# Fused attention and feed-forward: the first weight piece is loaded ahead of everything, and weight conversion runs one piece earlier

## The chip, the cores and the metric

The kernel runs on one core of one Trainium2 chip. The metric is the device time of one execution in microseconds (us). The time before is 648.15 us, the median of three runs (646.57 to 648.39).

## The reference

`B, H, S, D = 4, 8, 768, 64`. Attention looks at a window of keys and at one summary of each block of 32 keys; a feed-forward layer with the Mish function follows. All data are float32.

```python
k_sum = k.reshape(B, H, nb, 32, D).max(axis=3)
v_sum = v.reshape(B, H, nb, 32, D).mean(axis=3)
scores_l = scale * q @ k^T          # kept where |i - j| < 16, else -1e9
scores_s = scale * q @ k_sum^T + log(32)
a = softmax(concat([scores_l, scores_s]))
attn = a @ concat([v, v_sum])                 # (4, 8, 768, 64)
x = attn.transpose(0, 2, 1, 3).reshape(3072, 512)
h = x @ w_in                                   # 512 -> 2048
g = h * tanh(log1p(exp(h)))
out = g @ w_out                                # 2048 -> 512
```

## The kernel before

**Work and tiling.** Tokens are cut into 12 chunks of 256; an attention *unit* is one chunk with one of four pairs of heads, so there are 48 units. Two chunks (512 tokens) make one of six groups of the feed-forward. A group has 16 steps; step i does `ff_in` (12 matmuls into `ph`, L386), Mish on ScalarE (L393), a split of the result into a high part `ah` and a rest `al` (L402, L404), and, two steps later, `ff_out` (12 matmuls into `po`, L414). Every product is made of three matmuls on high and low parts.

**Weights.** Both weight matrices arrive as 64-bit floats and are converted on the chip. They are cut into 16 pieces, taken in turn from `w_in` and `w_out`; I call them p0 to p15. An even piece feeds two `ff_in` steps, an odd one two `ff_out` steps. Each piece goes through five calls, each of which takes the oldest piece that has finished the call before:

- `load_weight` (L122): two loads of 512 KB on SyncE's queue into one of two `stage` buffers. The load of the third piece therefore waits until the first has been begun, and so on, and whatever is queued behind it on SyncE waits with it.
- `begin_weight`: a copy `f` on ScalarE (L134) and two shifts on VectorE (L136, L138). This frees the stage buffer.
- `join_weight`: two operations on VectorE (L146, L148).
- `upper_weight`: the high part `w_hi` on ScalarE (L156).
- `lower_weight`: the low part `w_lo` on VectorE (L163).

**Order.** It is written by hand: every engine takes its instructions in the order of the program. First all loads of the first eight units are issued. Then a loop over u = 0 to 10 treats these units as a pipeline: scores of unit u (`sc` on TensorE, `pr` with L327 on VectorE, exponentials on ScalarE, L331), normalisation of unit u-1 (L341, L342 on VectorE, L343 on GpSimd), the value summary `vm` of unit u-1, the product with the values of unit u-3 (`x_ps`, with `xh` L373 on ScalarE and `xl` L374 on VectorE), and the transposes of unit u-2 (`pt`). `first_key_summary(hp)` (`km`, L242 on VectorE) must come before the scores of unit hp. The calls for the weights are put between these at chosen values of u. Then the main loop runs over the 96 steps; in its first steps it opens with

```python
upper_weight(); join_weight(); begin_weight(); load_weight()
if 0 < i <= NFC:
    waiting.pop(0)()      # al of step i-1
```

and `lower_weight()` follows after `ff_in` and the scores of a step. Later attention units are spread over these steps.

**Before.** In the loop over u the pieces go so: p0 is begun at u=1, joined at 2, lowered at 3; p1 begun at 6, joined at 8, lowered at 9; p2 begun at 8, joined at 10; p3 begun at 10. Step 0 of the main loop joins p3, begins p4, and lowers p2.

Of the kernel before, what the change touches and what calls it, by code (L numbers as in the profile page):

```python
# [30 lines left out]
HP = H // 2  # L31
# [26 lines left out]
def fused_kernel(ctx: ExitStack, tc: tile.TileContext, q0, qk, kt, v0, vw, vs, w_in, w_out, out):  # L58
# [45 lines left out]
    def home(j, part, dtype, name):  # L104

        if j == NW:
            t = stage.tile([P, WB, WP], I64, tag="stage", name=name).bitcast(dtype)
            return t.rearrange("p k f -> p (k f)")[:, :WB * WP]
        pool = const if j < EARLY else late[0]
        return pool.tile([P, WB * WP], dtype, tag=f"w{part}_{j}", name=name, bufs=1)  # L110
# [6 lines left out]
    def load_weight():  # L117
        if weights:
            w, fc = weights.pop(0)
            t = stage.tile([P, WB, WP], I64, tag="stage", name=f"w{w}_{fc}")  # L120
            for k in range(WB):
                nc.sync.dma_start(t[:, k, :], (w_in, w_out)[w][fc + k])  # L122
            loaded.append((w, fc, t))

    def begin_weight():
        if loaded:
            w, fc, t = loaded.pop(0)
            j = order[w, fc]
            flat = t.rearrange("p k f -> p (k f)")
            high = flat.bitcast(U32).rearrange("p (f two) -> p f two", two=2)[:, :, 1]  # L130
            quarter = flat.bitcast(U16).rearrange("p (f four) -> p f four", four=4)
            x = home(j, 0, U32, f"x{w}_{fc}")
            f = home(j + 1, 1, F32, f"f{w}_{fc}")
            nc.scalar.activation(f, high.bitcast(F32), AF.Copy, scale=2.0 ** -OFFSET)  # L134
            half = x.bitcast(U16).rearrange("p (f two) -> p f two", two=2)
            nc.vector.tensor_scalar(out=half[:, :, 0], in0=quarter[:, :, 1], scalar1=13, scalar2=None,  # L136
                                    op0=ALU.logical_shift_right)
            nc.vector.tensor_scalar(out=half[:, :, 1], in0=quarter[:, :, 3], scalar1=SIGN, scalar2=None,  # L138
                                    op0=ALU.bitwise_and)
            begun.append((w, fc, f, x))  # L140
# [64 lines left out]
    def first_keys(hp):  # L205

        ks = keys0[hp] = first_att.tile([P, WIN + S], F32, tag="ks", name=f"ks0_{hp}")
        nc.gpsimd.memset(ks[:, 0:WIN], 0.0)
        nc.sync.dma_start(ks[:, WIN:], kt[0, hp])
        t = first_att.tile([P, CH], F32, tag="q0", name=f"q0_{hp}")  # L210
        nc.sync.dma_start(t, q0[hp])
        t = t.rearrange("p (s q) -> p s q", s=NQ)
        units[0, hp] = {"q": [t, t], "k": ks[:, :CH + 2 * WIN]}

    def first_key_summary(hp):
        key_summary(0, hp, keys0[hp][:, WIN:])

    def window_values(c, hp):
        pool = first_att if c == 0 or (c < CG and hp > 1) else att
        u = units.setdefault((c, hp), {})  # L220
        u["v"] = pool.tile([KA, NQ, P], F32, tag="vw", name=f"vw{c}_{hp}", bufs=HP if pool is first_att else 2)
        nc.sync.dma_start(u["v"][0:KW], vw[c, hp].rearrange("p (s k) -> p s k", s=NQ))

    def block_values(c, hp):
        nc.gpsimd.tensor_copy(units[c, hp]["v"][KW:KA],
                              summary[c // CPB, hp][1].unsqueeze(1).broadcast_to([NB, NQ, P]))

    def second_queries(hp):
        t = first_att.tile([P, NQ, P], F32, tag="q1", name=f"q1_{hp}")
        nc.sync.dma_start(t, qk[1, hp].rearrange("p (s k) -> p s k", s=NQ)[:, :, :P])  # L230
        units[1, hp] = {"q": [t[:, :, h * QT:(h + 1) * QT] for h in range(2)], "k": keys0[hp][:, CH:]}

    def first_values(hp):
        window_values(0, hp)
        t = first_att.tile([P, NR, P], F32, tag="v0", name=f"v0_{hp}", bufs=HP)
        nc.sync.dma_start(t, v0[hp].rearrange("p (j d) -> p j d", d=P))
        units[0, hp]["rest"] = t

    def key_summary(b, hp, keys):

        km = att.tile([P, NB], F32, tag="km", name=f"km{b}_{hp}", bufs=HP)
        nc.vector.reduce_max(km, keys.rearrange("p (n j) -> p n j", j=BLK), axis=AX.X)  # L242
        summary[b, hp] = [km]

    def first_value_summary(hp):

        vm = att.tile([KA, P], F32, tag="vm", name=f"vm0_{hp}", bufs=HP)[KW:KA]
        summary[0, hp].append(vm)
        vwt, t = units[0, hp]["v"], units[0, hp]["rest"]
        ps = att_psum(0, f"vm_ps0_{hp}")  # L250
        for j in range(NQ + NR):
            nc.tensor.matmul(ps[KW:KA, 0:P], *((blocks[0:KW, j, :], vwt[0:KW, j, :]) if j < NQ else
                                               (blocks[:, j, :], t[:, j - NQ, :])),
                             start=(j == 0), stop=(j == NQ + NR - 1))
        nc.scalar.copy(vm, ps[KW:KA, 0:P])
        block_values(0, hp)
# [9 lines left out]
    def att_load_keys(c, hp):  # L266
        t = att.tile([P, NQ, P + KA], F32, tag="qk", name=f"qk{c}_{hp}")
        nc.sync.dma_start(t, qk[c, hp].rearrange("p (s k) -> p s k", s=NQ))
        units[c, hp] = {"qk": t}
# [67 lines left out]
    def att_normalize(group):  # L337
        n = len(group) * NQ
        u = units[group[0]]
        rs = small.tile([P, 2 * NQ], F32, tag="rs", name=f"rs{group[0][0]}_{group[0][1]}")[:, :n]  # L340
        nc.vector.tensor_scalar_add(rs, u["sm"][:, :n], 1e-9)  # L341
        nc.vector.reciprocal(rs, rs)  # L342
        nc.gpsimd.tensor_mul(u["pr"], u["pr"], rs.unsqueeze(2).broadcast_to([P, n, KA]))  # L343
# [11 lines left out]
    def att_values(group):  # L355
        c, hp0 = group[0]
        n = len(group)
        g, half = divmod(c, CG)
        if g not in xs:
            xs[g] = (xp.tile([P, HP, TG], F32R, tag="xh", name=f"xh{g}"),  # L360
                     xp.tile([P, HP, TG], F32R, tag="xl", name=f"xl{g}"))
        xh, xl = (x[:, hp0:hp0 + n, half * CH:(half + 1) * CH] for x in xs[g])
        ps = att_psum(c, f"x_ps{c}_{hp0}")
        for k, unit in enumerate(group):
            u = units.pop(unit)
            for s in range(NQ):
                for h in range(2):
                    d = slice(h * D, (h + 1) * D)
                    x = ps[d, k * CH + s * QT:k * CH + (s + 1) * QT]
                    pt = u["pt"][:, h * NQ // 2 + s // 2, s % 2 * QT:(s % 2 + 1) * QT]  # L370
                    nc.tensor.matmul(x, u["v"][:, s, d], pt, start=True, stop=True)  # L371
        x = ps[:, :n * CH].rearrange("p (k t) -> p k t", k=n)
        nc.scalar.copy(xh, x)  # L373
        return lambda: nc.vector.tensor_sub(xl, x, xh.bitcast(F32))  # L374
# [51 lines left out]
    todo = [(c, hp) for c in range(NCH) for hp in range(HP)]  # L426
# [8 lines left out]


    n = CG * HP
    first_keys(0)
    first_keys(1)
    load_weight()  # L440
    for hp in range(HP):
        first_values(hp)
        if hp + 2 < HP:
            first_keys(hp + 2)
    for hp in range(HP):
        second_queries(hp)
        if hp < 2:
            window_values(*todo[HP + hp])
        if hp == 1:
            load_weight()  # L450
    for unit in todo[n:n + 2]:
        att_load_keys(*unit)
    first_key_summary(0)
    for u in range(n + 3):
        if u < n:
            att_scores([todo[u]])
        if 1 <= u <= n:
            att_normalize([todo[u - 1]])
        if 1 <= u <= HP:
            first_value_summary(u - 1)  # L460
        lower = att_values([todo[u - 3]]) if 3 <= u else None
        if u in (3, 4):
            window_values(*todo[HP + u - 1])
        if HP < u <= n:
            block_values(*todo[u - 1])
        if 2 <= u < n + 2:
            att_transpose([todo[u - 2]])
        if u in (0, 2):
            first_key_summary(u + 1)
        if lower:  # L470
            lower()
        if u in (3, 9):
            lower_weight()
        if u in (2, 8, 10):
            join_weight()
            upper_weight()
        if u in (1, 6, 8, 10):
            begin_weight()
            load_weight()
        if u == 1:  # L480
            first_key_summary(u + 1)
        if u in (7, 8):
            att_load_values(*todo[u + 1])
# [108 lines left out]
```

## Time and profile before

| | |
|---|---|
| median of the runs | 648.15 us (646.57 to 648.39) |
| profiled execution, its time | 646.2 us |
| profiled execution, its span | 644.5 us |
| TensorE busy | 619.1 us (96%) |
| VectorE busy | 274.8 us (43%) |
| ScalarE busy | 276.8 us (43%) |
| GpSimd busy | 68.4 us (11%) |
| granted TensorE clock, mean | 0.992 |

PE is TensorE, PEld its weight load, DVE VectorE, ACT ScalarE, POOL GpSimd, SPq the queue of SyncE on which the transfers are issued. In a row of the timeline the columns are start, duration, engine, line, operation, output and input, count, and in brackets the idle time of that engine just before with what ended it. Instructions of one engine overlap a little in these rows, so the cost of one inside a chain is best read from its start to the start of the next.

### The profile page before, as it was taken

How to read it: one execution, taken by the hardware profiler on the slowest of the kernel's cores; microseconds unless marked ns; L12 is line 12 of the kernel's file. 1: busy time of each engine (PE TensorE's matmuls, PEld its weight loads, DVE VectorE, ACT ScalarE, POOL GpSimd, SP SyncE). 2: the span in 40 equal slices, each digit the busy share in tenths (PEclk: the TensorE clock that was granted, in tenths of full speed). 3: DMA queues.
4: the chain of work that ended last, by engine and by line, in shares of the span. 5: the costliest groups of instructions: out<-in, count | busy, mean ns of one | idle time of the engine just before them, and what ended most of it. 6: DMA issues, size and time to landing. Idle time of an engine off the chain costs nothing.

```text
span 644.5 us, 10836 instructions
## 1 busy us (share of the span) xinstructions
PE 619.1 (96%) x4224; PEld 508.4 (79%) x4224; DVE 274.8 (43%) x776; ACT 276.8 (43%) x662; POOL 68.4 (11%) x103
## 2 busy tenths in 40 slices
PE   5858999999999999999999999999999999999997
PEld 4746787788888888888888888888888888888886
DVE  4679999954323344523233254433233232222111
ACT  3759978655425424434245254254353342111111
POOL 4431010111001011011011011010110110000000
PEclk9969999999999999999999999999999999999999
DMA  8967698423404134422023244232231110100001
GB/s 273 317 192 249 241 290 267 124 94 112 142 2 119 64 106 145 149 61 95 3 93 95 91 144 139 80 95 85 76 95 41 54 32 1 66 0 2 1 0 65
DMA packets 31779, 69.27 MB, mean 107 GB/s; under 512 B 4720, under 2 KB 11120, under 8 KB 31728
## 3 DMA queue, kind: packets, MB, share of 16 engines
q1 hardware_dynamic: 31728, 68.58, 34.1%
q8 instruction: 33, 0.54, 0.4%
q14 instruction: 18, 0.15, 0.1%
HBM read 60.16 MB, written 6.29 MB: 103 GB/s over the span
## 4 chain that ended last, share of the span: by engine, by line
PE 87%; DMA 5%; DVE 5%; issue 2%; ACT 1%; POOL 0%; SPq 0%; DVEq 0%; POOLq 0%; ACTq 0%
PE po L414 40%; PE ph L386 37%; PE x_ps L371 4%; PE pt_ps L351 3%; PE sc L309 3%; DMA q<-qk 1%; DMA vw<-vw 1%; DVE x L136 1%; DMA vsum<-vs 1%; DMA w<-w_in 1%; DVE x L138 1%; DVE w_lo L163 1%; DMA ks<-kt 1%; DVE pr L327 1%; ACT pr L331 0%
## 5 line engine op out<-in xcount | busy, mean ns | idle before, releaser
L393 ACT ACTIVATE a<-ph 128x512 f32<-128x512 f32 x96 | 57.5, 599 | 252.1 <-PE ph L386 163.7
L414 PE MATMUL po<-w_hi,al 128*128 128x512 f32 x384 | 150.1, 391 | 3.6 <-DVE al L404 3.4
L386 PE MATMUL ph<-xh,w_lo 128*128 128x512 f32 x384 | 150.2, 391 | 2.0 <-DVE w_lo L163 2.0
L386 PE MATMUL ph<-xh,w_hi 128*128 128x512 f32 x384 | 152.2, 396 | 0.0
L414 PE MATMUL po<-w_hi,ah 128*128 128x512 f32 x384 | 151.9, 395 | 0.0
L386 PE MATMUL ph<-xl,w_hi 128*128 128x512 f32 x384 | 150.2, 391 | 0.0
L414 PE MATMUL po<-w_lo,ah 128*128 128x512 f32 x384 | 149.7, 390 | 0.0
L402 DVE CAST ah<-a 128x512 fp32r<-128x512 f32 x80 | 34.2, 428 | 226.1 <-ACT a L393 226.1
L414 PEld LDWEIGHTS po<-w_hi,al 128*128 128x128 f32 x384 | 72.1, 188 | 19.8 <-DVE al L404 5.5
L343 POOL TENSOR_TENSOR pr<-pr,rs 128x960 f32<-128x960 f32 (+1 forms) x28 | 44.3, 1583 | 404.9 <-DVE rs L342 388.4
L386 PEld LDWEIGHTS ph<-xh,w_lo 128*128 128x128 f32 x384 | 72.5, 189 | 17.7 <-DVE w_lo L163 2.5
L414 PEld LDWEIGHTS po<-w_hi,ah 128*128 128x128 f32 x384 | 72.0, 188 | 17.3 <-issue 3.0
L414 PEld LDWEIGHTS po<-w_lo,ah 128*128 128x128 f32 x384 | 72.2, 188 | 15.2
L386 PEld LDWEIGHTS ph<-xh,w_hi 128*128 128x128 f32 x384 | 72.6, 189 | 14.6 <-issue 0.2
L386 PEld LDWEIGHTS ph<-xl,w_hi 128*128 128x128 f32 x384 | 72.6, 189 | 14.5
L331 ACT ACTIVATE pr<-pr,nm 128x120 f32<-128x120 f32 x192 | 73.2, 382 | 13.6 <-DVE nm L327 13.4
L404 DVE TENSOR_TENSOR al<-a,ah 128x512 fp32r<-128x512 f32 x96 | 67.2, 700 | 5.6 <-ACT ah L402 2.9
L374 DVE TENSOR_TENSOR xl<-x_ps,xh 128x512 fp32r<-128x512 f32 (+1 forms) x28 | 17.2, 615 | 88.5 <-ACT xh L373 88.5
L353 ACT COPY pt<-pt_ps 120x512 f32<-120x512 f32 x48 | 26.2, 589 | 38.1 <-PE pt_ps L351 38.1
L371 PEld LDWEIGHTS x_ps<-pt,vw 120*64 120x64 f32 x768 | 25.6, 141 | 15.7 <-issue 9.4
L393 ACT ACT_TABLE_LOAD x21 | 26.9, 1283 | 24.8 <-PE ph L386 24.7
L371 PE MATMUL x_ps<-pt,vw 120*64 120x64 f32 x768 | 29.4, 229 | 7.0 <-POOL pr L343 4.5
(57 smaller groups left out, 479.5 us busy)
## 6 DMA issues: line engine op xcount, KB each, us to landing
qk<-qk SPq DMA_DIRECT2D x40, 496.0 KB, 4.2
vw<-vw SPq DMA_DIRECT2D x48, 192.0 KB, 4.9
w<-w_in SPq DMA_DIRECT2D x16, 512.0 KB, 5.3
w<-w_out SPq DMA_DIRECT2D x16, 512.0 KB, 5.7
ks<-kt SPq DMA_DIRECT2D x16, 384.0 KB, 4.5
out<-o SPq DMA_DIRECT2D x24, 256.0 KB, 2.3
vsum<-vs SPq DMA_DIRECT2D x12, 384.0 KB, 3.4
vw<-vm SPq DMA_DIRECT2D x40, 48.0 KB
```

The costliest lines, as they stand in the source:

```text
L309: nc.tensor.matmul(ps[h][row, at0:at0 + KA], u["qk"][r, s, h * QT:(h + 1) * QT], u["qk"][r, s, P:], start=True, stop=True)
L331: nc.scalar.activation(pr[:, j, :], pr[:, j, :], AF.Exp, scale=-1.0, bias=nm[:, j:j + 1], accum_out=sm[:, j:j + 1])
L343: nc.gpsimd.tensor_mul(u["pr"], u["pr"], rs.unsqueeze(2).broadcast_to([P, n, KA]))
L351: nc.tensor.transpose(ps[:KA, s * P:(s + 1) * P], u["p"][:, s, :], ident)
L353: nc.scalar.copy(u["pt"].rearrange("p s q -> p (s q)"), ps[:KA, :])
L371: nc.tensor.matmul(x, u["v"][:, s, d], pt, start=True, stop=True)
L374: return lambda: nc.vector.tensor_sub(xl, x, xh.bitcast(F32))
L386: nc.tensor.matmul(ph, w[:, cc * P:(cc + 1) * P], x[:, cc, :], start=(cc == 0 and n == 0), stop=(cc == NCC - 1 and n == 2))
L393: nc.scalar.activation(a, st[g, fc], AF.Mish)
L402: (nc.scalar.copy if g == 0 else nc.vector.tensor_copy)(ah, a)
L404: return lambda: nc.vector.tensor_sub(al, a, ah.bitcast(F32))
L414: nc.tensor.matmul(po[g][t], a[:, tok], w, start=(fc == 0 and n == 0), stop=(fc == NFC - 1 and n == 2))
```

## The change

Two things move; no instruction is added, taken out or altered.

- The loads: p0 is issued ahead of the keys of units 0 and 1 instead of behind them. p1 is issued behind the keys and queries of units 0 and 1 and the values of unit 0, instead of behind the second chunk's first two queries and windows. At that later place p0 is begun and p2 loaded.
- The conversion in the loop over u, now one piece further on: p0 joined at u=0, lowered at 1; p1 begun at 1, joined at 2, lowered at 3; p2 begun at 6, joined at 7, lowered at 8; p3 begun at 8, joined at 9; p4 begun at 10. Step 0 of the main loop joins p4, begins p5 and lowers p3. At u=0 the key summary of unit 1 comes behind the weight calls instead of ahead of them; at u=2 the summary of unit 3 stays ahead of them.

```diff
-    first_keys(0)
-    first_keys(1)
     load_weight()
     for hp in range(HP):
-        first_values(hp)
-        if hp + 2 < HP:
-            first_keys(hp + 2)
-    for hp in range(HP):
-        second_queries(hp)
-        if hp < 2:
-            window_values(*todo[HP + hp])
+        first_keys(hp)
+        if hp:
+            first_values(hp - 1)
         if hp == 1:
             load_weight()
+    first_values(HP - 1)
+    for hp in range(2):
+        second_queries(hp)
+        window_values(*todo[HP + hp])
+    begin_weight()
+    load_weight()
+    for hp in range(2, HP):
+        second_queries(hp)
...
-        if u in (0, 2):
-            first_key_summary(u + 1)
         if lower:
             lower()
-        if u in (3, 9):
+        if u == 2:
+            first_key_summary(u + 1)
+        if u in (1, 3, 8):
             lower_weight()
-        if u in (2, 8, 10):
+        if u in (0, 2, 7, 9):
             join_weight()
             upper_weight()
         if u in (1, 6, 8, 10):
             begin_weight()
             load_weight()
-        if u == 1:
+        if u < 2:
             first_key_summary(u + 1)
```

## The prediction

> **What bounds the kernel now.** I read the busy times by stage first, then TensorE's waits in the main loop, then VectorE's timeline from the start. The first rows are the span and three stages.
>
> ```profile
> span 644.5 us, 10836 instructions
> 0.00:52.00 52.00, 36.17 (x531) 29.03 (x532) 33.42 (x111) 31.21 (x94) 19.98 (x45) 0.90 0.81 246
> 52.00:119.00 67.00, 61.39 (x381) 48.90 (x380) 65.28 (x128) 55.59 (x105) 9.08 (x8) 1.00 0.83 273
> 119.00:644.50 525.50, 521.57 (x3315) 430.44 (x3314) 176.14 (x539) 189.99 (x465) 39.31 (x50) 1.00 0.24 73
> PE po L414 <- DVE al L404: 3.4, 3, 1.5
> PE ph L386 <- DVE w_lo L163: 2.0, 1, 2.0
> 118.77 0.50 PE L414 MATMUL po<-w_hi,al 128*128 128x512 f32 x1 [1.45 <-DVE al L404]
> ```
>
> The columns of a stage are its length, then the busy time of PE, PEld, DVE, ACT and POOL. From 119 us on TensorE is busy 521.57 of 525.5 us: it sets the pace, and nothing in the change touches that stage. From 52 to 119 VectorE is busy 65.28 of 67 us, and TensorE's only waits in the main loop, 3.4 + 2.0 = 5.4 us, are all for VectorE, the last one ending at 118.77. So the end of the program is about the time at which VectorE delivers that `al`, plus a fixed rest. Before 52 us VectorE is busy only 33.42 of 52 us; there it waits, in turn, for loads, TensorE and ScalarE. A change counts only by how it moves VectorE's chain up to 118 us.
>
> What one piece costs VectorE, in an undisturbed stretch:
>
> ```profile
> 49.93 0.69 DVE L146 TENSOR_SCALAR f<-f 128x1024 f32<-128x1024 f32 x1 [0.80 <-ACT f L134]
> 50.66 1.23 DVE L148 SCALAR_TENSOR_TENSOR f<-f,x 128x1024 uint32<-128x1024 uint32 x1
> 51.80 0.76 DVE L136 TENSOR_SCALAR x<-w 128x1024 uint16<-128x1024 uint16 x1
> 52.45 0.75 DVE L138 TENSOR_SCALAR x<-w 128x1024 uint16<-128x1024 uint16 x1
> 53.08 0.28 DVE L327 CUSTOM_DVE_ANT_0 pr<-sc,base 128x120 f32<-128x120 f32 x1
> 54.70 1.23 DVE L163 TENSOR_TENSOR w_lo<-f,w_hi 128x1024 fp32r<-128x1024 f32 x1
> 55.83 0.69 DVE L146 TENSOR_SCALAR f<-f 128x1024 f32<-128x1024 f32 x1
> ```
>
> From start to start, a join is 51.80 - 49.93 = 1.87 us, a begin 53.08 - 51.80 = 1.28, a lower 55.83 - 54.70 = 1.13: 4.28 us a piece. The `pr` of a pair of units takes 54.70 - 53.08 = 1.62.
>
> **The change, step 1: p0 ahead of the keys.** VectorE's first work now is `km` of unit 0, at 3.89 us when its keys land.
>
> ```profile
> 0.82 0.40 SPq L209 DMA_DIRECT2D ks<-kt  x1
> 3.89 0.95 DVE L242 TENSOR_REDUCE km<-ks 128x24 f32<-128x768 f32 x1 [3.89 <-DMA ks<-kt]
> 4.00:8.00 4.00, 2.40 (x34) 1.75 (x34) 2.49 (x10) 1.32 (x7) 1.50 (x8) 1.00 0.98 352
> 43.11 0.81 SPq L122 DMA_DIRECT2D w<-w_in  x2
> 43.50 4.87 DMA w<-w_in
> ```
>
> The last two rows are a piece loaded by itself: issued from 43.11, landed at 43.50 + 4.87 = 48.37, so 5.26 us in all. Issued at 0.82 instead, p0 lands at 6.08. The two shifts of its begin are ahead of `km` in VectorE's order: 6.08 + 1.28 = 7.36. The keys come behind 1.05 MB; at the 352 GB/s of the third row that moves them by 3.0 us, to 6.9, so they are not the later of the two. `km` starts 7.36 - 3.89 = **3.5 us later**. Ends: 3.0 (the loads alone, the shifts done meanwhile) and 5.3 (nothing of p0's load overlaps).
>
> The row of the transfers below shows that all loads share one queue. In the Trainium skill, "DMA: Bandwidth & Descriptors", section "Queues, rings and completion order", says that each engine of a queue takes its descriptors in ring order, so bytes put in front are paid by those behind. By that rule this term would be the 3.0 us of the loads or the 3.5 above, and never near nothing.
>
> ```profile
> q1 hardware_dynamic: 31728, 68.58, 34.1%
> ```
>
> **Step 2: p0 joined at u=0, lowered at u=1, p1 begun at u=1.** VectorE's order through the first units:
>
> ```profile
> 7.17 0.95 DVE L242 TENSOR_REDUCE km<-ks 128x24 f32<-128x768 f32 x1
> 10.62 0.73 DVE L136 TENSOR_SCALAR x<-w 128x1024 uint16<-128x1024 uint16 x1
> 10.86 1.31 POOL L343 TENSOR_TENSOR pr<-pr,rs 128x480 f32<-128x480 f32 x1 [5.17 <-DVE rs L342]
> 11.25 1.52 DVE L138 TENSOR_SCALAR x<-w 128x1024 uint16<-128x1024 uint16 x1
> 12.86 0.95 DVE L242 TENSOR_REDUCE km<-ks 128x24 f32<-128x768 f32 x1
> 17.13 0.93 DVE L146 TENSOR_SCALAR f<-f 128x1024 f32<-128x1024 f32 x1
> 18.09 1.52 DVE L148 SCALAR_TENSOR_TENSOR f<-f,x 128x1024 uint32<-128x1024 uint32 x1
> 19.54 0.27 DVE L327 CUSTOM_DVE_ANT_0 pr<-sc,first 128x120 f32<-128x120 f32 x1
> 22.93 0.42 DVE L374 TENSOR_TENSOR xl<-x_ps,xh 128x256 fp32r<-128x256 f32 x1 [2.21 <-ACT xh L373]
> 24.40 0.27 DVE L327 CUSTOM_DVE_ANT_0 pr<-sc,base 128x120 f32<-128x120 f32 x1
> 27.05 0.42 DVE L374 TENSOR_TENSOR xl<-x_ps,xh 128x256 fp32r<-128x256 f32 x1 [1.47 <-ACT xh L373]
> 22.77 0.42 PE L313 MATMUL sc<-ks,q 64*64 64x96 f32 x8 [1.42 <-DMA q<-qk]
> ```
>
> The `km` of unit 1 (7.17) releases that unit's scores, and so on: each unit waits for the one before it. The join of p0 now stands between `pr` of unit 0 and this `km`: +1.87. The lower of p0 is new at u=1 ahead of `km` of unit 2 (12.86): +1.13. The begin there took 12.86 - 10.62 = 2.24 us, beside GpSimd's 1.31 us at 10.86; now the lower runs beside GpSimd and the begin mostly after it, at 1.28. I give back 0.6 of the 0.96 (the join's second operation shows what a two-input operation loses there: 1.52 against 1.23, some 0.3). At u=2 a join stands as before (17.13 to 19.54), at u=3 a lower as before: nothing. The new ScalarE work here, a copy and a `w_hi`, lies in its waits for VectorE. Sum of steps 1 and 2: 3.5 + 1.9 + 1.1 - 0.6 = 5.9 us at `pr` of unit 3.
>
> On this overlap the Trainium skill, "SBUF — State Buffer", section "Who interferes with whom", speaks against the 0.6: an operation of VectorE with two inputs in SBUF contends with a GpSimd instruction that reads SBUF, and the loser blocks until the other is through. By it the lower would lose up to the 1.31 us of GpSimd's row and the sum would be 6.6 or more; the join beside GpSimd lost only 0.3, so I stay with the row.
>
> **Step 3: what passes on.** TensorE waited 1.42 us for unit 4's queries (22.77). The queries have 1.05 MB more ahead of them, while units 0 to 3 arrive 5.9 later, so this wait vanishes and TensorE's own path is late by only 5.9 - 1.4 = 4.5. But `pr` of unit 4 (24.40) hangs on `xl` and so on ScalarE (the waits of 2.21 and 1.47), which follows `pr` of unit 3 without slack. I take **5.6**, near the upper value; ends 4.5 and, with step 1's upper end, 7.7.
>
> **Step 4: the tail of the loop over u.** VectorE from `xl` of unit 4 to `xl` of unit 7, and the main loop to the first `al`:
>
> ```profile
> 36.68 0.42 DVE L374 TENSOR_TENSOR xl<-x_ps,xh 128x256 fp32r<-128x256 f32 x1 [1.04 <-ACT xh L373]
> 38.36 0.42 DVE L374 TENSOR_TENSOR xl<-x_ps,xh 128x256 fp32r<-128x256 f32 x1 [0.65 <-ACT xh L373]
> 43.38 0.43 DVE L374 TENSOR_TENSOR xl<-x_ps,xh 128x256 fp32r<-128x256 f32 x1 [0.95 <-ACT xh L373]
> 45.50 0.42 DVE L374 TENSOR_TENSOR xl<-x_ps,xh 128x256 fp32r<-128x256 f32 x1 [0.56 <-ACT xh L373]
> 45.84 0.69 DVE L146 TENSOR_SCALAR f<-f 128x1024 f32<-128x1024 f32 x1
> 47.82 1.05 ACT L156 CAST w_hi<-f 128x1024 fp32r<-128x1024 f32 x1 [2.35 <-DVE f L148]
> 58.98 0.69 DVE L404 TENSOR_TENSOR al<-a,ah 128x512 fp32r<-128x512 f32 x1
> ```
>
> Between these `xl` stood a join, a begin and a lower; now two joins, a begin and a lower. The join of p2 at u=7 may fill idle time (0.65 + 0.95 + 0.56 = 2.2 us). But each join has a `w_hi` behind it on ScalarE, 1.05 us, which waits for the join (47.82) and holds up the `xh` queued behind it; at u=9 that is `xh` of unit 7, which was behind no such wait before. I work out `xl` of unit 7 as 1.3 us later against its surroundings; ends 0 and 1.87 + 1.05 = 2.9.
>
> **Step 5: the reserve.** From 45.84 to the first `al` VectorE took 58.98 - 45.84 = 13.14 us: three joins, three begins, a `pr`, a lower and the wait of 0.80. Now: three begins (3.84), two joins (3.74), a `pr` (1.62) and a lower (1.13), 10.33 us: **2.8 less**. The wait of `ff_in` for `w_lo` (2.0) goes too, but `ff_out` behind it then waits the longer for `al`. After this the work per step is what it was, one piece further on, so VectorE stays the bound to 118 us and the lead is kept, not added to. The order of SyncE's loads in steps 0 on is as before; each load still waits for a begin two pieces back, and the vsum and qk loads behind it move along.
>
> **Sum.** 5.6 + 1.3 - 2.8 = **+4.1 us**. The profiled execution, 646.2 us, would be 650.3; it lies 2 us under the median of 648.15, against which I predict **652.3**. The likeliest case's own range is 650 to 656: 4.5 - 2.8 = +1.7, and 7.7 + 2.9 - 2.8 = +7.8.
>
> **The rivals.**
> *Only the loads pass on.* The join and lower at u=0 and 1 hide in the 18.6 us (52 - 33.42) in which VectorE idles early, and the shift is the 3.0 of the loads; with 1.3 - 2.8 that is +1.5: 649.7, within 0.3% (1.9 us, about what can be told from no change). For it: the idle time, and the 1.42 at unit 4. Against it: the idle time lies after the `km` and before `xl`, not where the new work stands.
> *The reserve removes all waits.* If VectorE's chain ceases to be the bound in the main loop, the whole 5.4 us of waits go; with the loads' 3.0 that is -2.4: 645.7, faster. It decides once VectorE's lead over TensorE exceeds the longest wait (2.0) at every step and the start loses under 3.5. For it: every wait is for VectorE. Against it: 65.28 of 67 us busy leave it no time to gain a lead, and the piece taken out of that stretch is one join.
> *The change does nothing of what it says* is not to be had for the loads; for the reserve it would be if p2's load waited on its stage buffer, but p0 is begun at about 7 us, before the second piece is even issued.
>
> **How the numbers follow.** The forecast has 0.66, its rarer upper cases included; only the loads, 0.20; the reserve, 0.14. Slower 0.68 (a few of the middle cases end above 650.1), same 0.18, faster 0.14. The range 646.5 to 655.5 leaves out about 0.11 below and 0.09 above.
>
> **What the profile after would show.** Right: first `km` near 7.4 us; the `km` of unit 1 some 5.4 later than 7.17; no wait for `q<-qk` at unit 4; `pr` of unit 4 near 30; no wait of `ph` for `w_lo`; the first `al` near 63; VectorE still full to about 123, with a wait of `po` for `al` near there. Wrong if the first `km` starts by 5, if `pr` of unit 4 is at 27 or earlier, or if TensorE has no waits in the main loop.

## The result, and the profile after

The changed kernel takes 651.2 us in the median (650.74 to 651.7, five runs), the kernel before 647.64 on the same chip: ratio 1.0059, 95% interval 1.0041 to 1.0076, so 3.8 us slower (2.7 to 4.9). The prediction was +4.1 (652.3 against 648.15). The profiled execution took 650.74 us with a span of 649.0, 4.5 us over both of before.

First two stages of the changed kernel, the second cut 4 us later than before so that it holds about the same work; then TensorE's waits in the main loop, and the last of them.

```profile
0.00:52.00 52.00, 32.02 (x483) 25.69 (x484) 33.18 (x110) 29.38 (x92) 20.96 (x45) 0.87 0.73 244
56.00:123.00 67.00, 63.20 (x417) 50.58 (x409) 65.31 (x128) 55.67 (x104) 9.06 (x8) 1.00 0.77 258
PE po L414 <- DVE al L404: 4.0, 3, 1.6
123.34 0.50 PE L414 MATMUL po<-w_hi,al 128*128 128x512 f32 x1 [1.43 <-DVE al L404]
```

The 67 us behind the start look as they did: VectorE 65.31 us busy, where it was 65.28. The wait of `ph` for `w_lo` is gone, the waits for `al` grew from 3.4 to 4.0, and the last ends at 123.34 instead of 118.77, 4.57 later. Behind it nothing changed: 649.0 - 123.34 = 525.66 us are left, before it was 644.5 - 118.77 = 525.73. The first `al` is late by the same 4.57, so the whole loss is made ahead of it, and VectorE's timeline shows where:

```profile
5.90 0.74 DVE L136 TENSOR_SCALAR x<-w 128x1024 uint16<-128x1024 uint16 x1 [5.90 <-DMA w<-w_in]
7.16 0.94 DVE L242 TENSOR_REDUCE km<-ks 128x24 f32<-128x768 f32 x1
10.42 0.69 DVE L146 TENSOR_SCALAR f<-f 128x1024 f32<-128x1024 f32 x1
12.28 0.95 DVE L242 TENSOR_REDUCE km<-ks 128x24 f32<-128x768 f32 x1
15.73 1.20 DVE L163 TENSOR_TENSOR w_lo<-f,w_hi 128x1024 fp32r<-128x1024 f32 x1
16.84 1.53 DVE L136 TENSOR_SCALAR x<-w 128x1024 uint16<-128x1024 uint16 x1
18.90 0.93 DVE L242 TENSOR_REDUCE km<-ks 128x24 f32<-128x768 f32 x1
25.61 0.28 DVE L327 CUSTOM_DVE_ANT_0 pr<-sc,first 128x120 f32<-128x120 f32 x1 [0.77 <-PE sc L315]
29.99 0.28 DVE L327 CUSTOM_DVE_ANT_0 pr<-sc,base 128x120 f32<-128x120 f32 x1
52.91 0.42 DVE L374 TENSOR_TENSOR xl<-x_ps,xh 128x256 fp32r<-128x256 f32 x1 [1.38 <-ACT xh L373]
63.55 0.67 DVE L404 TENSOR_TENSOR al<-a,ah 128x512 fp32r<-128x512 f32 x1
```

Against the rows of before, the same instruction is late by 7.16 - 3.89 = 3.27 us at the first `km`, 12.28 - 7.17 = 5.11 at the second, 18.90 - 12.86 = 6.04 at the third, 25.61 - 19.54 = 6.07 at `pr` of unit 3, 29.99 - 24.40 = 5.59 at `pr` of unit 4, 52.91 - 45.50 = 7.41 at `xl` of unit 7, and 63.55 - 58.98 = 4.57 at the first `al`. From there the lateness stays what it is.

### The profile page after: what moved, and what is told of

Read it like the earlier page. It is cut to its first block, busy times and chain, and to the rows that moved or that the text cites. A ratio compares the mean times of both kernels' runs of the same rounds, so it can differ in the third digit from the quotient of the medians.

```text
span 649.0 us, 10833 instructions
## 1 busy us (share of the span) xinstructions
PE 621.1 (96%) x4224; PEld 509.7 (79%) x4224; DVE 273.0 (42%) x776; ACT 276.9 (43%) x662; POOL 68.8 (11%) x103
## 4 chain that ended last, share of the span: by engine, by line
PE 87%; DVE 8%; issue 2%; DMA 2%; ACT 1%; SPq 0%; DVEq 0%; ACTq 0%
PE po L414 39%; PE ph L386 37%; PE x_ps L371 3%; PE pt_ps L351 3%; PE sc L309 3%; DVE x L136 1%; DVE w_lo L163 1%; DVE x L138 1%; PE vm_ps L252 1%; DVE pr L327 1%; DMA vsum<-vs 1%; DVE f L146 1%; ACT pr L331 1%; DMA w<-w_in 1%; DVE f L148 1%
```

## Experiments

All times are given as the ratio to the kernel before in runs on the same chip, with its 95% interval, and as the us that the ratio makes of 647 us. A row of a profile is one execution, and executions differ: `xl` of unit 0 stands at 22.93 us in the kernel before, and at 23.58 and 22.54 in two kernels below (nothing converted in step 0; no low parts) whose program is the same up to there; with the changed kernel's start it stands between 28.22 and 29.77 in three kernels. Rows of two profiles that differ by less than about 1 us therefore show little; what a change is worth is read from the ratios.

### p0's load alone

```diff
-    first_keys(0)
-    first_keys(1)
     load_weight()
+    first_keys(0)
+    first_keys(1)
```

> Only p0's load is moved ahead of the keys; the conversion stays as before. Theory (every us by which VectorE's chain starts late reaches the end, unless TensorE's wait at unit 4 takes it up): the first km starts about 3.0 us later (1.05 MB at 352 GB/s), near 6.9; unit 4's queries have the same bytes ahead of them as before, so TensorE's 1.42 us wait there shrinks, but pr of unit 4 is still some 3 us late; no reserve is gained, so the whole is about +2.7 us (+1.6 to +3.0) against before, near 650.3. Rival (the loads are hidden, only the added conversion at u=0 and 1 costs): 647.6, no change.

Ratio 1.0028 (1.0017 to 1.0039), +1.8 us. VectorE's chain in this kernel:

```profile
6.73 0.95 DVE L242 TENSOR_REDUCE km<-ks 128x24 f32<-128x768 f32 x1 [6.73 <-DMA ks<-kt]
25.05 0.42 DVE L374 TENSOR_TENSOR xl<-x_ps,xh 128x256 fp32r<-128x256 f32 x1 [2.21 <-ACT xh L373]
61.16 0.68 DVE L404 TENSOR_TENSOR al<-a,ah 128x512 fp32r<-128x512 f32 x1
```

The first `km` is 2.84 us late, close to the 3.0 of 1.05 MB; 2.12 is left at `xl` of unit 0 (22.93 before) and 2.18 at the first `al`; TensorE's last wait for `al` ends at 121.73, 2.96 late. So the load in front is not hidden: 1.1 to 2.5 us of it reach the end by the ratio. Whether slack on the way takes up any of the 2.84 is not settled, as the last row is late by all of it.

### The changed kernel's loads, the old conversion

```diff
-        if u in (1, 3, 8):
+        if u in (3, 9):
             lower_weight()
-        if u in (0, 2, 7, 9):
+        if u in (2, 8, 10):
             join_weight()
             upper_weight()
-        if u in (1, 6, 8, 10):
+        if u in (6, 8, 10):
             begin_weight()
```

(against the changed kernel; the key summaries are also back in their old places)

> The changed kernel's loads and the begin of p0 ahead of the loop, but everything else of the conversion where it was before (p0 joined at u=2, lowered at 3, p1 begun at 6). Theory: the first km is 3.3 us late as in the changed kernel, the begin of 2.2 us is gone from u=1, so pr of unit 3 is only about 1.1 us late; then unit 4's queries, with 1.05 MB more ahead of them, are the gate: TensorE waits for them until 25.6 to 26.5, about +3.4 on TensorE's path, and the end is +2 to +3.5 against before, 649.6 to 651.1. Rival (only VectorE's order counts): +1.1, 648.7. If the loads are hidden altogether: 645.4, since 2.2 us left the chain.

Ratio 1.0013 (1.0000 to 1.0026), +0.8 us: the rival's value, and my theory is wrong here. TensorE did not wait for unit 4's queries at all: the first row below is its scores of unit 4, with no wait in front, at 22.62, where before it was 22.77 after a wait of 1.42. The second row is the same scores in the kernel without low parts further down (lines are 3 further on there): its loads are those of before, and it has no such wait either. The rows after these are the first 30 us of this kernel, of the kernel before, and of that same kernel without low parts; the last column is GB/s.

```profile
22.62 0.42 PE L313 MATMUL sc<-ks,q 64*64 64x96 f32 x8
20.92 0.42 PE L316 MATMUL sc<-ks,q 64*64 64x96 f32 x8
0.00:30.00 30.00, 18.81 (x320) 15.66 (x320) 15.51 (x69) 15.76 (x57) 11.25 (x35) 1.00 0.98 322
0.00:30.00 30.00, 20.91 (x351) 17.07 (x352) 16.80 (x70) 16.89 (x62) 12.43 (x37) 1.00 0.98 289
0.00:30.00 30.00, 21.84 (x351) 17.82 (x352) 16.74 (x70) 17.22 (x62) 13.15 (x37) 0.96 0.98 310
```

So the wait of 1.42 was a matter of that one execution, and the expectation that unit 4's queries become the gate fails. With p0 and p1 moved forward, the same busy share of the transfers (0.98) carries 322 GB/s instead of 289, 1 MB more in 30 us; but 310 were reached in the old order too, so how much of this is the order is open. The new order of the loads costs 0.8 us when p0's begin is out of u=1. The other 3 us of the change come from the conversion.

### VectorE's order at u=0 and u=1

```diff
-        if u == 2:
+        if u < 3:
             first_key_summary(u + 1)
...
-        if u < 2:
-            first_key_summary(u + 1)
```

> The changed kernel, but the key summaries of units 1 and 2 are ahead of the weight calls of u=0 and u=1 (only VectorE's order changes). Theory (the join and the lower of p0 and the begin of p1 cost as much as they do because the next unit's scores wait for a km behind them): VectorE then works on the weight while it would wait for scores (gaps of 1.39 and 0.87 us in the changed kernel), so pr of unit 3, at 25.61, is 2 to 2.8 us earlier and the end 2 to 2.8 us earlier than the changed kernel, 648.4 to 649.2. Rival (the loads at the start are the cost): as the changed kernel, 651.2.

Ratio 1.0025 (1.0006 to 1.0044), +1.6 us (0.4 to 2.8): by the ratios 2.2 us less than the changed kernel, as expected, though each of the two ratios is known only to about 1.2 us. Nothing but the order of a few instructions differs.

```profile
10.42 0.95 DVE L242 TENSOR_REDUCE km<-ks 128x24 f32<-128x768 f32 x1
14.24 0.92 DVE L242 TENSOR_REDUCE km<-ks 128x24 f32<-128x768 f32 x1
22.51 0.27 DVE L327 CUSTOM_DVE_ANT_0 pr<-sc,first 128x120 f32<-128x120 f32 x1
60.99 0.68 DVE L404 TENSOR_TENSOR al<-a,ah 128x512 fp32r<-128x512 f32 x1
62.95 1.23 DVE L163 TENSOR_TENSOR w_lo<-f,w_hi 128x1024 fp32r<-128x1024 f32 x1 [1.28 <-ACT w_hi L156]
122.44 0.50 PE L414 MATMUL po<-w_hi,al 128*128 128x512 f32 x1 [0.80 <-DVE al L404]
```

The `km` of units 1 and 2 come 1.86 and 4.66 us earlier than in the changed kernel, `pr` of unit 3 3.1 us earlier, the first `al` 2.56. The join, lower and begin are now done while VectorE would wait for scores. Not all of it lasts in this profile: behind the first `al` VectorE waits 1.28 us for a `w_hi` of ScalarE, and TensorE's last wait ends at 122.44, only 0.90 earlier than in the changed kernel. So what the first steps of the change cost is in good part not the work, but that it stands ahead of the next unit's `km`; 2.2 us is the best estimate of that part, and the last row of the profile shows 0.9.

### The tail: the high part of p3 behind `xh` of unit 7

```diff
             join_weight()
+        if u in (0, 2, 7, 10):
             upper_weight()
```

> The changed kernel, but the high part of p3 on ScalarE is issued at u=10, behind xh of unit 7, instead of at u=9 ahead of it. Theory (this wait makes the tail late and VectorE is the bound behind it): xl of unit 7, at 52.91 in the changed kernel, is about 1.2 us earlier, and so are the first al and the end: 650.0. Rival (the tail is not on the path): 651.2, with the first al at 63.5 as it is.

Ratio 1.0065 (1.0046 to 1.0084), +4.2 us (3.0 to 5.4): the expected gain of 1.2 us is not seen. `xl` came earlier as expected, the end did not:

```profile
51.29 0.42 DVE L374 TENSOR_TENSOR xl<-x_ps,xh 128x256 fp32r<-128x256 f32 x1
62.76 0.68 DVE L404 TENSOR_TENSOR al<-a,ah 128x512 fp32r<-128x512 f32 x1
92.13 1.22 DVE L262 TENSOR_REDUCE vq<-vsum 96x32 f32<-96x1024 f32 x1 [2.24 <-DMA vsum<-vs]
97.33 0.50 PE L414 MATMUL po<-w_hi,al 128*128 128x512 f32 x1 [1.33 <-DVE al L404]
```

`xl` of unit 7 is 1.62 us earlier (0.16 of it already at unit 6, at 49.11 instead of 49.27), the first `al` only 0.79, and at 92 us VectorE waits 2.24 us for a load of `vsum` (0.87 in the changed kernel). In this profile a new wait for `al` at 97.33 follows, the last wait ends at 124.41, 1.07 later than in the changed kernel, and the gain is gone. Why this load landed later here was not settled.

### A reserve alone, and drawn on

Three kernels. The first is the kernel before with step 0 of the main loop converting nothing:

```diff
-        upper_weight()
-        join_weight()
-        begin_weight()
-        load_weight()
+        if i:
+            upper_weight()
+            join_weight()
+            begin_weight()
+            load_weight()
```

> The kernel before, but step 0 of the main loop does not upper, join, begin or load, so that all pieces from p3 on come one step later: the reserve that the kernel before already has is drawn on, and nothing is paid at the start. Theory (VectorE is the bound to the first al only as far as TensorE's scores let it run ahead): 3.15 us of a join and a begin leave VectorE's chain, 1.4 to 1.8 of it counts as in the run with the changed kernel; TensorE's wait of 2.0 for w_lo and the al waits shrink, the end is 1 to 2.5 us earlier than before, near 645.5. Rival (this lead is needed): new waits of ph for w_lo in later steps, 648 or more.

Ratio 1.0041 (1.0022 to 1.0059), +2.7 us: wrong, the rival holds. The lead of before was needed:

```profile
PE ph L386 <- DVE w_lo L163: 6.7, 5, 2.7
PE po L414 <- DVE al L404: 1.0, 2, 0.8
```

TensorE's waits for `al` fell from 3.4 to 1.0 us, but those for `w_lo` rose from 2.0 to 6.7, 2.3 more in all. The profiled execution was the longest of seven (653.26 us, the median is 649.62), so these two rows show which waits came, not what they cost in a usual one.

The second leaves the main loop alone and puts one more piece into what I took for VectorE's idle time:

```diff
+        if u == 4:
+            begin_weight()
+            load_weight()
+        if u == 5:
+            clip_weight()       # first half of join_weight
+        if u == 6:
+            merge_weight()      # second half
+        if u == 7:
+            upper_weight()
+        if u == 8:
+            lower_weight()
         if lower:
             lower()
```

> The kernel before with its loads and its first three steps, but one more piece is converted in VectorE's idle time: p1 begun at u=4, joined half at 5 and half at 6, upper at 7, lowered at 8, each ahead of xl; all later pieces move one on, so the main loop starts with the same reserve as in the changed kernel. Theory (what cost time is the place of the conversion, and a reserve of a whole piece buys nothing by itself as the work behind xl of unit 7 is then the same as before): no change from before within 1 us, 647.3 to 648.3, first al about 13 us behind xl of unit 7. Rival (the reserve is worth the 2.8 us that I gave it): 644.5.

The third is the second with the skip of the first:

> As the run with one more piece converted in VectorE's idle time, and step 0 of the main loop does not upper, join, begin or load. Theory: the reserve is drawn on, first al some 2 to 3 us nearer to xl of unit 7, the end 1 to 2.5 us earlier than before, near 645.5, and no wait of ph for w_lo. Rival (the reserve does not matter, only the start does): as without the skip, 647.3 or more.

The second has ratio 1.0053 (1.0037 to 1.0068), +3.4 us; the third 1.0002 (0.9989 to 1.0015), no change. The rows are `xl` of unit 7 and the first `al` of the second kernel, a wait at its u=4, then `xl` and `al` of the third (lines are 11 further on in these two).

```profile
48.15 0.43 DVE L385 TENSOR_TENSOR xl<-x_ps,xh 128x256 fp32r<-128x256 f32 x1 [0.56 <-ACT xh L384]
61.62 0.67 DVE L415 TENSOR_TENSOR al<-a,ah 128x512 fp32r<-128x512 f32 x1
26.23 0.75 DVE L136 TENSOR_SCALAR x<-w 128x1024 uint16<-128x1024 uint16 x1 [1.12 <-DMA w<-w_out]
50.88 0.42 DVE L385 TENSOR_TENSOR xl<-x_ps,xh 128x256 fp32r<-128x256 f32 x1 [0.55 <-ACT xh L384]
62.21 0.67 DVE L415 TENSOR_TENSOR al<-a,ah 128x512 fp32r<-128x512 f32 x1
```

With a whole piece more in reserve and the same tail, the first `al` comes 61.62 - 48.15 = 13.47 us behind `xl`, as before (13.48): the reserve by itself buys nothing. Drawn on, it is 11.33, and by the ratios the kernel is 3.3 us faster than without the skip. The profiles do not show that gain at the first `al`, 62.21 against 61.62: the third's execution was its longest of twelve, and `xl` of unit 7 came 2.73 us later in it although the two programs are the same up to there. Both expected times were missed, "no change" by the second and 1 to 2.5 us less than before by the third, for the extra piece made `xl` of unit 7 2.65 us late in the second and 5.38 in the third: the idle time was not free, partly because the loads of the pieces were not there (1.12 us at u=4).

The changed kernel, which has this reserve, was tried with the same skip:

> The changed kernel, but step 0 of the main loop does not upper, join, begin or load; all pieces from p4 on come one step later there, which is the lead that the kernel before had. Theory (VectorE bounds 56 to 123 us, and a reserve counts only when it is drawn on): 3.15 us (a join and a begin) leave VectorE's chain ahead of the first al, and a whole piece ahead of the last waiting al; TensorE's waits of 4.0 us for al shrink to under 1.5 us, and the end is 3 to 4 us earlier, 647.2 to 648.2. Rival (TensorE and the loads set the stage): 651.2. Rival (the reserve is needed): new waits of ph for w_lo, 652 or more.

Ratio 1.0052 (1.0033 to 1.0072), +3.4 us, not to be told from the changed kernel: the expected gain of 3 to 4 us did not come. VectorE had nothing to do with the time that it was given:

```profile
58.38 0.28 DVE L327 CUSTOM_DVE_ANT_0 pr<-sc,base 128x120 f32<-128x120 f32 x1 [2.36 <-PE sc L309]
50.00:57.00 7.00, 6.22 (x29) 4.78 (x28) 4.61 (x8) 4.26 (x5) 0.16 (x1) 0.50 0.55 187
```

It waited 2.36 us for the scores of step 0, behind an `ff_in` that TensorE ran at a granted clock of 0.50 (second row). The first `al` stood 9.99 us behind `xl` of unit 7, against 10.64 in the changed kernel. So 3.15 us of VectorE's work taken out gave 0.65 there. (In this execution `xl` of unit 7 was also 1.40 us later than in the changed kernel, at 54.31, although the edit comes behind it.)

Two more kernels kept the third kernel above and moved loads, to take away its waits for p1 and p2:

> As the run with one more piece converted in VectorE's idle time and nothing converted in step 0, with only the keys of the main loop's first units moved behind p2 in the loads. Theory: the wait for p2 at u=6 (2.3 us) goes, the one for p1 at u=4 stays: 0.5 to 2 us earlier than before, 645 to 646.5. Rival (the loads are not on the path): 647.1.

> As the run with one more piece converted in VectorE's idle time and nothing converted in step 0, and the loads rearranged: p1 behind the values of unit 2, and the keys of the main loop's first units (1 MB) behind p2. In that run VectorE waited 1.4 us for p1 at u=4 and 2.3 us for p2 at u=6. Theory: both waits go, nothing else is late, the end is 1 to 2.5 us earlier than that run and than before, 644.6 to 646. Rival (p1's megabyte delays the queries of unit 4 and with them the rest): 647 or more.

Ratios 0.9989 (0.9972 to 1.0007) and 1.0003 (0.9985 to 1.0021): neither can be told from the kernel before, and neither expected gain came. The waits for p1 and p2 did shrink: to 0.53 and nothing in the first, to nothing in the second. In their place VectorE waited 2.32 and 2.37 us for the scores of step 0 (1.83 in the third kernel above), as in the run before. No version tried that computes the whole reference beats the kernel before.

### What VectorE's relief is worth at most

This kernel leaves out the low parts of all pieces but the first two, so it does not compute the reference.

```diff
-            nc.vector.tensor_sub(split[w, fc, 1], f, split[w, fc, 0].bitcast(F32))
+            if order[w, fc] < 2:
+                nc.vector.tensor_sub(split[w, fc, 1], f, split[w, fc, 0].bitcast(F32))
+            else:
+                split[w, fc, 1] = split[w, fc, 0]
```

> The kernel before without the low parts of p2 to p15: lower_weight issues nothing for them and TensorE multiplies by the high part twice. 14 times 1.13 us leave VectorE, nothing else changes for TensorE. It bounds what any relief of VectorE can bring: if VectorE is the only cause of TensorE's waits in the main loop, all 5.4 us of them go but for the last one, which a load of vsum may hold: -4 to -5.4 us, 642 to 643.3. If TensorE is bound otherwise: 647.3.

Ratio 0.9950 (0.9934 to 0.9966), -3.2 us (-4.3 to -2.2), a little less than expected. One wait in the main loop is left, of 2.2 us for the first `al`:

```profile
PE po L417 <- DVE al L407: 2.2, 1, 2.2
```

5.4 - 2.2 = 3.2 us of waits went, and that is what the kernel gained. VectorE does bound TensorE in this stage, but only by these waits: with the start as it is, relieving VectorE can win at most the 5.4 us of them, and whether the last 2.2 can go is not shown. The changed kernel paid 5.6 at the start.

## Why the prediction was right, step by step

The signs named in advance for the profile after are there: the first `km` at 7.16, that of unit 1 5.11 later than before, no wait for unit 4's queries, `pr` of unit 4 at 29.99, no wait of `ph` for `w_lo`, the first `al` at 63.55, the last wait for `al` ending at 123.34.

**Step 1** (+3.5): 3.27 measured; p0 landed at 5.9 instead of 6.08, and its two shifts took the 1.26 us that were put ahead of `km`. The run with the load alone shows 2.84 of it to be the bytes. The trace agrees with the ring order that the Trainium skill gives ("DMA: Bandwidth & Descriptors", section "Queues, rings and completion order"): the megabyte in front made the keys behind it 2.84 us late.

**Step 2** (+1.9, +1.1, -0.6): the join measured 12.28 - 10.42 = 1.86, the lower 16.84 - 15.73 = 1.11, but the begin took 18.90 - 16.84 = 2.06, so only 0.18 came back, not 0.6. GpSimd and VectorE did get in each other's way, as the Trainium skill ("SBUF — State Buffer", section "Who interferes with whom") has it, but the lower was not the loser for which I had drawn on it:

```profile
15.97 1.80 POOL L343 TENSOR_TENSOR pr<-pr,rs 128x480 f32<-128x480 f32 x1 [10.30 <-DVE rs L342]
```

GpSimd started 0.24 us behind the lower and took 1.80 us instead of 1.31; the lower, begun first, lost nothing (1.20 against 1.23), and the first shift behind it lost the 0.8 us (1.53 against 0.74). The shift has one input, a case that the sentence drawn on does not speak of; that GpSimd is the cause is read from the overlap of the rows, and no run takes GpSimd away. The sum of steps 1 and 2 was forecast as 5.9 and is 6.04 at the third `km`, nearer to that than to the 6.6 of the rule. At `pr` of unit 3, for which the 5.9 was given, 6.07 is in part luck: at `pr` of unit 2 the lateness is only 20.70 - 15.19 = 5.51, and the other 0.56 came while VectorE waited 0.77 us for a slow TensorE (last section), for which the prediction had no term. That the order is a good part of the cost is shown by the run with `km` ahead: 2.2 us of the 3.8 go by the ratios.

**Step 3** (5.6 passes on): 5.59. The value held, a reason beside it did not. TensorE does not wait for unit 4's queries in the changed kernel, but neither does it in other executions with the loads of before (20.92, no wait), so the 1.42 us were no property of the kernel and the lower end of 4.5 rested on one execution. That the queries are 1.05 MB later is not borne out: with the new loads and the old conversion TensorE had its scores at 22.62 without a wait. It did no harm, as VectorE's chain was later still. The main reason, that `pr` of unit 4 hangs on `xl` and so on ScalarE, fits the rows: `xl` of unit 0, at 28.52 instead of 22.93, is late by the same 5.59.

**Step 4** (+1.3): 7.41 - 5.59 = 1.82, half a us more, inside the ends given. From `xl` to `xl` the lateness is 5.44 at unit 4, 7.74 at unit 5, 5.89 at unit 6 and 7.41 at unit 7. The mechanism, a `w_hi` ahead of `xh` of unit 7, is borne out by `xl` of that unit coming 1.62 us earlier when it is moved; that this time counts at the end is not, since the run with it moved was no faster.

**Step 5** (-2.8): 7.41 - 4.57 = 2.84. The size was right, the word reserve was not. What shortened this stretch is that a join moved from behind `xl` of unit 7 to ahead of it; the lead of one piece with the same work behind `xl` left the stretch at 13.47.

**Sum:** 5.59 + 1.82 - 2.84 = 4.57 against 4.1 forecast, in the profile; 3.8 by the ratio. That single terms come this close is partly luck, as executions with the same start differ by 1 us and more at `xl` of unit 0. The rival of the hidden conversion, +1.5, falls with the measured 2.7 to 4.9; with `km` ahead the conversion does hide for the most part, and the time is +1.6. The rival in which the reserve removes all waits falls with the 4.0 us of waits still there.

## What to carry to other kernels

In this kernel, work moved into the start-up phase was cheap or dear by what was queued behind it on its engine: ahead of the instruction that the next unit waits for, a join and a lower cost their whole length; behind it, part of the work was free. The idle time of VectorE there was mostly waiting inside a chain, and filling it moved the chain. A lead of one piece, with VectorE doing the same work in every step, was worth nothing until a step was allowed to do less. It is worth asking of another kernel whether it is built the same way.

## What the runs showed of the hardware that I had not expected

- ScalarE's table load stands directly in front of p0's copy, its first function, and started only when p0 had landed:

```profile
5.87 1.28 ACT L134 ACT_TABLE_LOAD   x1 [5.87 <-DMA w<-w_in]
```

  Before, a load of the same length stood at 0.81 us, while ScalarE had nothing else. Here it put the copy at 7.16; the join came 3 us later, so it cost nothing.
- TensorE slowed down in the late start: from 16 to 24 us the granted clock was 0.82 in the changed kernel, where the kernel before had 1.00 up to 36 us. The second half of unit 1's `vm` took 1.91 us (1.04 before) and held up `pr` of unit 3 by 0.77 us:

```profile
16.00:24.00 8.00, 6.43 (x60) 4.66 (x59) 7.06 (x17) 3.85 (x15) 3.79 (x3) 0.82 1.09 308
21.78 1.91 PE L252 MATMUL vm_ps<-v,blocks 128*24 128x128 f32 x8
```

  The granted clock of the rows is not the whole of it: in the changed kernel with nothing converted in step 0 the two halves took 1.90 and 1.92 us at a granted clock of 1.00 from 20 to 24 us. What the slow executions share is that TensorE had waited 3.8 us for the `km` of unit 1; with `km` ahead that wait was 1.55 and the halves took 1.05 and 1.04.

- At the same busy share the rate of the loads over the first 30 us was not the same: with the loads of before 289 GB/s, and 279 and 310 in two other kernels; with the changed kernel's loads 317 to 328 in five kernels, and 325 already with p0 alone in front. The order seems to matter, but the 30 us also hold other transfers, and executions of one order differ by 31 GB/s:

```profile
0.00:30.00 30.00, 19.00 (x307) 15.58 (x309) 15.65 (x64) 15.01 (x53) 11.57 (x35) 1.00 0.98 325
```
